# Seven products of sums of quarters in place of eight: the second matrix product of a gated feed-forward layer behind a packed attention

## The chip, the cores and the metric

The kernel runs on one core of one Trainium2 chip. The metric is the device time of one execution in microseconds, the median of three runs. Work is spread by hand over TensorE (PE, and PEld for its weight loads), VectorE (DVE), ScalarE (ACT) and the DMA queue that SyncE (SP) issues. GpSimd makes an identity matrix at the start and is idle after that.

## The reference, cut to what matters

```python
def sm_attn(qq, kk, vv):
    s = scale * np.matmul(qq, kk.transpose(0, 1, 3, 2))
    a = np.exp(s - np.max(s, axis=-1, keepdims=True))
    return np.matmul(a / (np.sum(a, axis=-1, keepdims=True) + 1e-09), vv)
# q, k, v: (8 batches, 8 heads, 576, 64); p: (8, 8, 32, 64)
p_packed = sm_attn(p, k, v)
x = sm_attn(q, p_packed, p_packed)      # as rows: (8 * 576, 512)
h = x @ w_in                            # w_in: (512, 2048)
g = h * np.tanh(np.log1p(np.exp(h)))    # mish
out = g @ w_out                         # w_out: (2048, 512)
```

All inputs come in 64 or 32 bits; the two weight matrices come as 64-bit floats and are turned into 32-bit ones in the kernel.

## The kernel before

A batch has 576 rows: four chunks of 128 and 64 left over. Since the attention has only 32 packed positions per head, w_in is first multiplied by the packed values (`pack`, L711), which gives 256 rows of weights for the batch, and the up product (`Group.up`, L800) multiplies these by the attention weights `aT`. Each of the 16 groups of a batch makes 128 of the 2048 hidden columns: two halves of 288 rows, six products each, since every operand stands as a high and a low part and three of the four cross products are kept. I call these products **ups**. ScalarE applies mish from PSUM to SBUF (`gate`, L810), VectorE makes the high part (`high`, L818) and the low part (`low`, L822).

The second product (`Group.down`, through `down_one`, L852 to L854) takes a 128x128 block of g as the stationary operand and 512 columns of w_out as the moving one. For each group and each of the four chunks it runs three products of 512 columns: high by high, high by low, low by high. I call these **downs**. Four PSUM banks hold the four chunks through the 16 groups of a batch; then `keep` (L841 to L845) copies each bank to SBUF and a DMA sends it. The 64 left rows of two batches are put side by side and multiplied by w_out once per four groups (`Left`, `ps_rest`, 48 products of 512 columns for a pair of batches).

w_out stays in SBUF all along as 16 tiles `wo` of high and low parts. w_in in 32 bits lies in DRAM (`w_in_f32`) and is fetched again for each batch.

Batches 0 and 1 run as three turns (half of batch 0, batch 1, the other half of batch 0), since the weights arrive and are converted during them; batches 2 to 7 run one after the other. The attention of the next batch (`later`) is interleaved with the groups of this one.

The order of instructions on every engine is fixed. The class `Lineup` is given each operation with an engine, an assumed cost, what it reads and which slots of which buffers it holds, and puts the operations in order; the kernel is written out in this order. Each engine runs its own list strictly in turn and waits where an operand or a buffer is late. The slots are named pools: `acc` (four PSUM banks for the second product), `ps_h`, `ps_x` and `ps_a` (PSUM for ups, scores and packs), `g` (mish output), `gs` (split g), `T`, `late`, `wstage`, `w32`.

## Time and profile before

| | |
|---|---|
| median of three runs | 721.99 us (721.77 to 722.18) |
| the profiled execution's own time | 722.63 us |
| its span, first to last instruction | 720.9 us |
| TensorE busy | 698.6 us, 97% of the span |
| VectorE busy | 394.4 us, 55% |
| ScalarE busy | 301.8 us, 42% |
| moved by DMA | 85.75 MB, mean 119 GB/s |

Busy time of TensorE is modelled: matmuls are pipelined and their recorded durations overlap, so the distance between two starts says what a product costs, and the chain of waits (what released what, followed back from the end) says how much of a stretch each line accounts for. An engine that is idle off that chain costs nothing.

### The profile page before, as it was taken

What the parts mean: (1) busy time and instruction counts of PE and PEld (TensorE: products, weight loads), DVE (VectorE), ACT (ScalarE), POOL (GpSimd) and SP (SyncE); (2) the same over time, 40 slices, a digit from 0 to 9 for tenths busy, and PEclk for the clock granted to TensorE, in tenths of its full rate; (3) what the DMA queues carried; (4) which work ended last, traced back from release to release, by engine and by line L of the source; (5) the groups of instructions that cost most, each with busy time, mean ns of one, the idle gap of its engine ahead of it and who ended that gap; (6) DMA issues with size and microseconds to landing.
All of it is one profiled execution on the core that took longest, in us unless ns stands there. A gap on an engine that the chain in (4) does not pass through costs nothing.

```text
span 720.9 us, 12533 instructions
## 1 busy us (share of the span) xinstructions
PE 698.6 (97%) x5050; PEld 571.4 (79%) x5050; DVE 394.4 (55%) x711; ACT 301.8 (42%) x718; POOL 0.7 (0%) x6
## 2 busy tenths in 40 slices
PE   5599999999999999999999999999999999999997
PEld 4278888777788788878888788887878878787885
DVE  5899878957544473355632555453643438332332
ACT  5598766565222443233422443334423344223211
POOL 0000000000000000000000000000000000000000
PEclk8879999999999999999999999999999999999999
DMA  9990255813047301641017310373016430130002
GB/s 316 363 371 3 88 150 203 292 60 117 5 135 256 118 1 59 207 159 75 1 59 282 129 43 1 108 273 117 1 26 220 150 117 1 59 117 1 1 1 73
DMA packets 29754, 85.75 MB, mean 119 GB/s; under 512 B 3584, under 2 KB 7680, under 8 KB 29696
## 3 DMA queue, kind: packets, MB, share of 16 engines
q1 hardware_dynamic: 29696, 84.95, 34.0%
q8 instruction: 40, 0.66, 0.4%
q14 instruction: 18, 0.15, 0.1%
HBM read 71.30 MB, written 13.63 MB: 118 GB/s over the span
## 4 chain that ended last, share of the span: by engine, by line
PE 93%; DMA 4%; ACT 1%; DVE 0%; issue 0%; SPq 0%
PE ps_h L800 28%; PE acc L852 17%; PE acc L853 16%; PE acc L854 16%; PE ps_w L711 4%; DMA xT<-in_k_main_dram 2%; PE ps_rest L852 2%; PE ps_rest L853 2%; PE ps_rest L854 2%; PE ps_m L302 1%; DMA w_st<-in_w_in_dram 1%; PE ps_pp L430 1%; PE ps_s L302 1%; DMA v_rest<-in_v_rest_dram 1%; PE ps_a L395 1%; PE ps_pp L445 0%
## 5 line engine op out<-in xcount | busy, mean ns | idle before, releaser
L810 ACT ACTIVATE g<-ps_h 128x288 f32<-128x288 f32 (+1 forms) x256 | 97.5, 386 | 310.6 <-PE ps_h L800 158.5
L852 PE MATMUL acc<-wo,g_hi 128*128 128x512 f32 x512 | 206.6, 404 | 0.0
L853 PE MATMUL acc<-wo,g_hi 128*128 128x512 f32 x512 | 202.2, 395 | 0.0
L854 PE MATMUL acc<-wo,g_lo 128*128 128x512 f32 x512 | 201.3, 393 | 0.0
L818 DVE CAST g_hi<-g 128x512 fp32r<-128x512 f32 x112 | 47.6, 425 | 212.5 <-PE acc L853 159.7
L800 PE MATMUL ps_h<-aT_hi,wp_hi 128*128 128x288 f32 x512 | 152.0, 297 | 0.3 <-ACT g L810 0.3
L800 PE MATMUL ps_h<-aT_hi,wp_lo 128*128 128x288 f32 x512 | 151.5, 296 | 0.0
L800 PE MATMUL ps_h<-aT_lo,wp_hi 128*128 128x288 f32 x512 | 151.4, 296 | 0.0
L852 PEld LDWEIGHTS acc<-wo,g_hi 128*128 128x128 f32 x512 | 96.2, 188 | 31.9 <-issue 20.1
L854 PEld LDWEIGHTS acc<-wo,g_lo 128*128 128x128 f32 x512 | 96.2, 188 | 22.5
L800 PEld LDWEIGHTS ps_h<-aT_hi,wp_hi 128*128 128x128 f32 x512 | 96.6, 189 | 13.4 <-issue 1.0
L853 PEld LDWEIGHTS acc<-wo,g_hi 128*128 128x128 f32 x512 | 96.3, 188 | 10.8
L800 PEld LDWEIGHTS ps_h<-aT_lo,wp_hi 128*128 128x128 f32 x512 | 96.7, 189 | 9.7
L800 PEld LDWEIGHTS ps_h<-aT_hi,wp_lo 128*128 128x128 f32 x512 | 96.6, 189 | 0.0
L822 DVE TENSOR_TENSOR g_lo<-g,g_hi 128x512 fp32r<-128x512 f32 x128 | 88.0, 688 | 9.0 <-DVE g_hi L818 0.5
L737 DVE TENSOR_TENSOR wp_lo<-ps_w,wp_hi 128x512 fp32r<-128x512 f32 x64 | 42.4, 686 | 14.7 <-ACT wp_hi L732 12.5
L732 ACT CAST wp_hi<-ps_w 128x512 fp32r<-128x512 f32 x64 | 35.3, 595 | 25.8 <-PE ps_w L711 24.9
L711 PE MATMUL ps_w<-wi,ppT 64*32 64x512 f32 x512 | 33.1, 597 | 0.0
L812 ACT ACTIVATE g_rest<-ps_h 128x64 f32<-128x64 f32 x128 | 28.5, 222 | 0.0
L852 PE MATMUL ps_rest<-wo,r_hi 128*128 128x512 f32 x64 | 25.1, 393 | 0.0
L853 PE MATMUL ps_rest<-wo,r_hi 128*128 128x512 f32 x64 | 25.1, 393 | 0.0
L854 PE MATMUL ps_rest<-wo,r_lo 128*128 128x512 f32 x64 | 25.1, 392 | 0.0
(96 smaller groups left out, 553.5 us busy)
## 6 DMA issues: line engine op xcount, KB each, us to landing
wi<-w_in_f SPq DMA_DIRECT2D x48, 512.0 KB, 5.1
w_st<-in_w_in_dram SPq DMA_DIRECT2D x16, 512.0 KB, 7.2
xT<-in_k_main_dram SPq DMA_DIRECT2D x16, 512.0 KB, 6.2
v<-in_v_main_dram SPq DMA_DIRECT2D x16, 512.0 KB, 6.6
xT<-in_q_main_dram SPq DMA_DIRECT2D x16, 512.0 KB, 7.5
w_st<-in_w_out_dram SPq DMA_DIRECT2D x16, 512.0 KB, 7.8
out_dram<-o SPq DMA_DIRECT2D x32, 256.0 KB, 2.2
w_in_f<-wi SPq DMA_DIRECT2D x8, 512.0 KB, 6.5
```

The costliest lines, as they stand in the source:

```text
L302: nc.tensor.matmul(out=out[u][h * NP:(h + 1) * NP], lhsT=packT[u * D:(u + 1) * D, h * NP:(h + 1) * NP], rhs=xT[u * D:(u + 1) * D, h * (e - ...
L711: nc.tensor.matmul(out=ps[g][h * NP:(h + 1) * NP], lhsT=ppTb[row:row + D, g, h * NP:(h + 1) * NP], rhs=wis[c, g][row:row + D, h // 2, :], ...
L732: nc.scalar.copy(out=hi, in_=fresh[b, c][g])
L737: nc.vector.tensor_tensor(out=lo, in0=fresh[b, c][g], in1=hi.bitcast(F32), op=ALU.subtract)
L800: nc.tensor.matmul(out=ps, lhsT=w[:, fs], rhs=a[:, g, cs], start=(n == 0), stop=(n == 5))
L810: nc.scalar.activation(out=self.act[:, hf * HALF:hf * HALF + m], in_=ps[:, :m], func=AF.Mish)
L812: nc.scalar.activation(out=self.g_rest[self.b % 2, self.f // 4][:, self.f % 4, :], in_=ps[:, m:], func=AF.Mish)
L818: cast(out=self.g[0], in_=self.act)
L822: nc.vector.tensor_tensor(out=lo, in0=self.act, in1=hi.bitcast(F32), op=ALU.subtract)
L852: nc.tensor.matmul(out=acc, lhsT=hi[:, cs], rhs=wh, start=start, stop=False)
L853: nc.tensor.matmul(out=acc, lhsT=hi[:, cs], rhs=wl, start=False, stop=False)
L854: nc.tensor.matmul(out=acc, lhsT=lo[:, cs], rhs=wh, start=False, stop=stop)
```

## The change

From batch 2 on (`PLAIN = 2`) the second product is made in steps. A step takes 256 rows (half of the four chunks of a batch) and 256 hidden columns, and sees g as 2x2 blocks of 128x128 and w_out as 2x2 blocks of 128x256. In place of eight block products it makes seven, of sums and differences of the blocks (the scheme of Strassen and Winograd), each as three products of 256 columns. The seven sums accumulate over the eight steps of a half batch in three and a half PSUM banks (`BANKS`), and at the end of the half batch eight operations (`ending`: one copy on ScalarE, seven additions on VectorE) combine them into two output chunks. I call the seven times three products of 256 columns of a step its downs as well.

For each step the ups of both hidden blocks run over 256 rows in the first half of a batch and over 320 in the second (256 and the left 64). VectorE then makes four sums of blocks in three operations (`sums`), ScalarE the high parts of seven blocks at once (`high`, 896 columns), VectorE their low parts (`low`, 896 columns).

The blocks of w_out and their differences are made once: the conversion also stores w_out in 32 bits and its quarters to DRAM, `Mix` reads it back, makes the differences, splits and stores them, and `fetch_mix` brings 512 KB tiles into 18 slots (`u`). A half batch uses 28 of them. Steps go through w_out forwards in one half and backwards in the next, so that 18 of the 28 stay across the turn and ten are fetched per half batch. The left rows use the same tiles (`LeftMixed`, 24 products of 256 columns each, for two row blocks at once).

Besides: the pools get other sizes (two slots `T` for k and q in place of four; v shares five slots with w_in; GB 4), the sign of a converted weight is taken by an operation with one tensor in place of one with two, and the exponentials of batches 2 to 7 are taken from PSUM with their sums on ScalarE, as batches 0 and 1 have it, in place of a subtraction, an exponential and a sum over SBUF.

```diff
-GB = 3
-PAIRS = 8
-STAGED = 100
-AHEAD = 0
-XB = 4
-VB = 2
+LATER = 3
+GB = 4
+PLAIN = 2
+XB = 2
+WV = 5
+UB = 18
+WB = 4
+SB = 4
...
-    wo = {i: const.tile([P, 2, DO], F32R, name=f"wo{i}") for i in range(NF // 2)}
+    wo = {}
...
+    mixed = [[dram.tile([P, 2, 2, DO // 2], F32, name=f"mixed{p}_{k}") for k in range(3)] for p in range(NF // 2)]
+    shared = [dram.tile([P, 2, 2, DO // 2], F32, name=f"shared{j}") for j in range(NF // 4)]
...
+        def sign(self):
+            self.r = wts.tile([P, FC], I32, name="wround", tag="w2k", bufs=W2K)
+            nc.vector.tensor_scalar(out=self.r, in0=self.high, scalar1=-0x80000000, scalar2=None, op0=ALU.bitwise_and)
...
+            low = self.r.bitcast(U16).rearrange("p (n t) -> p n t", t=2)[:, :, 0]
+            nc.scalar.activation(out=low, in_=self.lower.bitcast(U32), func=AF.Copy, scale=2.0 ** -29)
...
+        def keep_f32(self):
+            nc.sync.dma_start(out=w_out_f32[self.i // 2][:, self.i % 2], in_=self.dst)
...
+        def keep_quarters(self):
+
+            p, w, half = self.i // 2, wo[self.i], DO // 2
+            nc.sync.dma_start(out=mixed[p][2][:, self.i % 2], in_=w[:, :, :half].bitcast(F32))
+            if self.i % 2:
+                nc.sync.dma_start(out=shared[p // 2][:, p % 2], in_=w[:, :, half:].bitcast(F32))
...
+        def differences(self):
+            half = DO // 2
+            self.t = wts.tile([P, 4, half], F32, name="mix_t", tag="st", bufs=SB)
+            w, t = self.w.rearrange("p i (u m) -> p (i u) m", u=2), self.t
+            nc.vector.tensor_tensor(
+                out=t[:, 0:2], in0=w[:, 1:2].to_broadcast([P, 2, half]), in1=w[:, 0:4:3], op=ALU.subtract
+            )
+            nc.vector.tensor_tensor(out=t[:, 2], in0=w[:, 3], in1=t[:, 0], op=ALU.subtract)
+            nc.vector.tensor_tensor(out=t[:, 3], in0=w[:, 2], in1=t[:, 2], op=ALU.subtract)
...
+    def fetch_mix(p, k):
+        x = wts.tile([P, 2, 2, DO // 2], F32R, name="mix", tag="u", bufs=UB)
+        if k < 3:
+            mixes[p, k] = x
+            nc.sync.dma_start(out=x.bitcast(F32), in_=mixed[p][k])
+        else:
+            others[p // 2] = x
+            nc.sync.dma_start(out=x.bitcast(F32), in_=shared[p // 2])
...
+            for q in range(2):
+                for half, terms in enumerate((((0, "w11"), (1, "w21")), ((2, "w22"), (0, "t3")))):
+                    for m, (x, name) in enumerate(terms):
+                        three(
+                            self.ps[:, half * DO // 2:(half + 1) * DO // 2], self.hi[:, q, x], self.lo[:, q, x],
+                            quarter(2 * self.i + q, name), q == 0 and m == 0 and half == 0, q == 1 and m == 1 and half == 1,
+                        )
...
+    def three(acc, hi, lo, w, start, stop):
+
+        nc.tensor.matmul(out=acc, lhsT=hi, rhs=w[:, 0], start=start, stop=False)
+        nc.tensor.matmul(out=acc, lhsT=hi, rhs=w[:, 1], start=False, stop=False)
+        nc.tensor.matmul(out=acc, lhsT=lo, rhs=w[:, 0], start=False, stop=stop)
...
+        X = {"s4": 0, "s2": 1, "s3": 2, "s1": 3, "x12": 4, "x22": 5, "x11": 6, "x21": 7}
+        BANKS = (
+            (("x11", "w11"), ("x12", "w21")),
+            (("s2", "t2"), ("s3", "t3")),
+            (("s1", "t1"), ("s4", "w22")),
+            (("x22", "t4"),),
+        )
...
+            a, e = ((0, MAIN // 2), (MAIN // 2, S))[self.hf]
...
+        def sums(self):
+            x = self.x
+            nc.vector.tensor_tensor(out=x[:, 3], in0=x[:, 7], in1=x[:, 5], op=ALU.add)
+            nc.vector.tensor_tensor(
+                out=x[:, 1:3], in0=x[:, 3:8:4], in1=x[:, 6:7].to_broadcast([P, 2, P]), op=ALU.subtract
+            )
+            nc.vector.tensor_tensor(out=x[:, 0], in0=x[:, 4], in1=x[:, 1], op=ALU.subtract)
...
+            nc.scalar.copy(out=self.split[:, 0], in_=self.x[:, :7])
...
+            nc.vector.tensor_tensor(out=x[:, 1], in0=self.x[:, :7], in1=x[:, 0].bitcast(F32), op=ALU.subtract)
...
+            for n, (x, w) in enumerate(self.BANKS[k]):
+                at = self.X[x]
+                three(
+                    sums[k][:, n * DO // 2:(n + 1) * DO // 2], self.split[:, 0, at], self.split[:, 1, at],
+                    quarter(self.p, w), self.first and n == 0, self.last and n == len(self.BANKS[k]) - 1,
+                )
...
+            if n == 0:
+                nc.scalar.copy(out=k1, in_=m1)
+                return
+            out_, a, c = (
+                (o[0][:, 0], m2, k1), (u2, m6, k1), (u3, m7, u2), (u4, m5, u2), (o[1][:, 1], m5, u3),
+                (o[0][:, 1], m3, u4), (o[1][:, 0], m4, u3),
+            )[n - 1]
+            nc.vector.tensor_tensor(out=out_, in0=a, in1=c, op=ALU.add)
...
-    turns = TURNS + [(b, 0, NF) for b in range(2, B)]
+    turns = TURNS
...
+    steps = [
+        Step(b, hf, p if hf == 0 else NF // 2 - 1 - p, p == 0, p == NF // 2 - 1)
+        for b in range(PLAIN, B) for hf in range(2) for p in range(NF // 2)
+    ]
...
-                later(b, b < 2)
+                later(b, True)
...
+                elif at == 0:
+                    for p in range(5, 8):
+                        mixed_in(p, p == 6)
+                elif x.first:
+                    for p in (2, 1, 0):
+                        mixed_in(p, p == 1)
```

Three places in the order of instructions. TensorE near the start, between the second scores (`ps_s`) and the first ups (`ps_h`); `ps_t` are the transposes that turn the attention weights of batch 0, `ps_a` and `ps_pp` belong to the attention of batch 1. Before:

```order
L302 MATMUL ps_s_371<-xT,pT 32x320 x4
L545 MATMUL ps_t<-ident,a_310 128x128 x8
L395 MATMUL ps_a_454<-ident,a_366 128x128 x4
L395 MATMUL ps_a_455<-ident,a_366 128x128 x4
L399 MATMUL ps_a_454<-ident,a_366 128x128
L545 MATMUL ps_t<-ident,a_310 128x128
L430 MATMUL ps_pp<-v,a1T 32x64 x32
L445 MATMUL ps_pp<-v_rest,a1T_rest 32x64 x8
L800 MATMUL ps_h<-aT_hi,wp_hi 128x288
```

and now:

```order
L310 MATMUL ps_s_452<-xT,pT 32x256 x4
L310 MATMUL ps_s_453<-xT,pT 32x320 x4
L310 MATMUL ps_s_452<-xT,pT 32x256 x4
L310 MATMUL ps_s_453<-xT,pT 32x320 x4
L912 MATMUL ps_h<-aT_hi,wp 128x288
```

The first ups now stand right behind the scores of batch 1; the transposes and the values of batch 1 come after three halves of ups.

VectorE at the end of a batch before (the banks `acc_2499` and `acc_2501` are the two that VectorE copies):

```order
L818 CAST g_hi<-g 128x512
L822 TENSOR_TENSOR g_lo<-g,g_hi 128x512
L818 CAST g_hi<-g 128x512
L822 TENSOR_TENSOR g_lo<-g,g_hi 128x512
L845 COPY o<-acc_2499 128x512
L845 COPY o<-acc_2501 128x512
L818 CAST g_hi<-g 128x512
L822 TENSOR_TENSOR g_lo<-g,g_hi 128x512
```

and now at the end of the first half of batch 2 (`acc_2725`, `acc_2772`, `acc_2779` and `acc_2813` are its banks 0 to 3; `at` and `aT_lo` belong to the attention of batch 3):

```order
L1063 TENSOR_TENSOR o<-acc_2725,o 128x256
L622 STREAM_TRANSPOSE at<-a_3089 128x576
L1025 TENSOR_TENSOR x<-x 128x128
L1026 TENSOR_TENSOR x<-x 128x256
L1029 TENSOR_TENSOR x<-x 128x128
L1063 TENSOR_TENSOR o<-acc_2772,o 128x256
L631 TENSOR_TENSOR aT_lo<-at,aT_hi 128x576
L1063 TENSOR_TENSOR o<-acc_2772,o 128x256
L622 STREAM_TRANSPOSE at<-a_3089 128x576
L1063 TENSOR_TENSOR o<-acc_2779,o 128x256 x3
L631 TENSOR_TENSOR aT_lo<-at,aT_hi 128x576
L1063 TENSOR_TENSOR o<-acc_2813,o 128x256
```

In place of two copies stand seven additions, some of which read what an earlier one wrote, with parts of the attention and of the next step between them.

TensorE at the same turn, where `acc_3259` is bank 0 of the next half batch:

```order
L972 MATMUL acc_2772<-mix,mixed_split 128x256
L973 MATMUL acc_2772<-mix,mixed_split 128x256
L974 MATMUL acc_2772<-mix,mixed_split 128x256
L972 MATMUL acc_2779<-mix,mixed_split 128x256
L973 MATMUL acc_2779<-mix,mixed_split 128x256
L974 MATMUL acc_2779<-mix,mixed_split 128x256
L972 MATMUL acc_2779<-mix,mixed_split 128x256
L973 MATMUL acc_2779<-mix,mixed_split 128x256
L974 MATMUL acc_2779<-mix,mixed_split 128x256
L972 MATMUL acc_3259<-mix,mixed_split 128x256
L973 MATMUL acc_3259<-mix,mixed_split 128x256
L974 MATMUL acc_3259<-mix,mixed_split 128x256
```

The next half's first downs follow at once; bank 1 of the next half (`acc_3274`) comes 15 products behind the last one into `acc_2772`, bank 2 comes 27 behind the last one into `acc_2779`.

## Rows read from the trace of the kernel before

**Rows 1.** Windows by stage: per engine busy us (instructions), clock, DMA share, GB/s.
```profile
core 0: us, PE busy (x) PEld busy (x) DVE busy (x) ACT busy (x) POOL busy (x), PEclk, DMA share, GB/s
0.00:41.50 41.50, 24.66 (x326) 15.51 (x327) 29.39 (x68) 23.40 (x55) 0.70 (x6) 0.78 0.98 346
41.50:226.80 185.30, 184.75 (x1252) 151.20 (x1252) 136.13 (x247) 107.07 (x242) 0.00 (x0) 1.00 0.43 146
226.80:397.20 170.40, 170.40 (x1262) 140.53 (x1268) 83.70 (x146) 62.76 (x151) 0.00 (x0) 1.00 0.31 109
```

**Rows 2.** Chain that ended last, 226.8 to 397.2 us, by line.
```profile
by line: PE ps_h L800 29.8%; PE acc L852 18.6%; PE acc L853 17.5%; PE acc L854 17.4%; PE ps_w L711 4.4%; PE ps_rest L852 2.2%; PE ps_rest L853 2.2%; PE ps_rest L854 2.2%; PE ps_s L302 1.6%; PE ps_m L302 1.5%; PE ps_pp L430 1.2%; PE ps_a L39
```

**Rows 3.** Groups by form: times run, busy us, mean ns, idle before.
```profile
L852 PE MATMUL acc<-wo,g_hi 128*128 128x512 f32 x512 | 206.6, 404 | 0.0
L800 PE MATMUL ps_h<-aT_hi,wp_hi 128*128 128x288 f32 x512 | 152.0, 297 | 0.3 <-ACT g L810 0.3
L800 PEld LDWEIGHTS ps_h<-aT_lo,wp_hi 128*128 128x128 f32 x512 | 96.7, 189 | 9.7
```

**Rows 4.** Timeline at 247.63 us: start us, us, what.
```profile
247.63 1.03 PE L395 MATMUL ps_a<-ident,a 128*128 128x128 f32 x8
248.51 0.27 PE L399 MATMUL ps_a<-ident,a 128*128 128x128 f32 x1
```

**Rows 5.** Groups by form: the work behind an up and at batch's ends.
```profile
L818 DVE CAST g_hi<-g 128x512 fp32r<-128x512 f32 x112 | 47.6, 425 | 212.5 <-PE acc L853 159.7 <-ACT g_rest L812 37.4 <-ACT g L810 11.2
L822 DVE TENSOR_TENSOR g_lo<-g,g_hi 128x512 fp32r<-128x512 f32 x128 | 88.0, 688 | 9.0 <-DVE g_hi L818 0.5
L605 DVE TENSOR_TENSOR aT_lo<-ps_t,aT_hi 128x128 fp32r<-128x128 f32 x1 | 0.3, 283 | 0.0
L760 DVE TENSOR_TENSOR r_lo<-g_rest,r_hi 128x256 fp32r<-128x256 f32 x32 | 12.1, 419 | 7.0 <-ACT r_hi L756 7.0
L508 DVE TENSOR_TENSOR a<-a,small 128x1152 f32<-128x1152 f32 x7 | 9.5, 1357 | 0.2
L810 ACT ACTIVATE g<-ps_h 128x288 f32<-128x288 f32 x128 | 53.0, 414 | 217.7 <-issue 147.2 <-PE ps_h L800 65.7 <-ACT wp_hi L732 2.9
L818 ACT CAST g_hi<-g 128x512 fp32r<-128x512 f32 x16 | 10.2, 637 | 1.5 <-PE acc L853 1.4
L618 ACT CAST aT_hi<-at 128x576 fp32r<-128x576 f32 x14 | 9.4, 675 | 6.8 <-DVE at L612 6.8
```

**Rows 6.** Timeline before the first up, 31.16 to 41.50 us.
```profile
31.16 1.42 DVE L588 TENSOR_TENSOR a<-a,small 128x512 f32<-128x512 f32 x2
32.95 0.67 ACT L645 ACTIVATE wi<-w_st 128x512 f32<-128x512 f32 x1 [3.35 <-DMA w_st<-in_w_in_dram]
...
35.60 1.97 PE L395 MATMUL ps_a<-ident,a 128*128 128x128 f32 x8 [1.68 <-ACT a L364]
37.73 0.42 DVE L652 TENSOR_SCALAR wi<-wi 128x512 f32<-128x512 f32 x1
40.48 0.28 DVE L605 TENSOR_TENSOR aT_lo<-ps_t,aT_hi 128x128 fp32r<-128x128 f32 x1
41.50 0.61 PE L800 MATMUL ps_h<-aT_hi,wp_hi 128*128 128x288 f32 x1
```

**Rows 7.** The page's DMA: rate by slice of 18 us, queue, landing.
```profile
GB/s 316 363 371 3 88 150 203 292 60 117 5 135 256 118 1 59 207 159 75 1 59 282 129 43 1 108 273 117 1 26 220 150 117 1 59 117 1 1 1 73
q1 hardware_dynamic: 29696, 84.95, 34.0%
wi<-w_in_f SPq DMA_DIRECT2D x48, 512.0 KB, 5.1
```

**Rows 8.** Timeline of the end.
```profile
715.66 0.39 PE L854 MATMUL acc<-wo,g_lo 128*128 128x512 f32 x1
716.08 0.69 DVE L845 COPY o<-acc 128x512 f32<-128x512 f32 x1 [0.67 <-PE acc L854]
716.20 1.52 SPq L848 DMA_DIRECT2D out_dram<-o  x3
```

More of the change, by code (lines that the diff above doesn't have):

```diff
@@ L836, in keep @@
             elif before is None:
-                o = parts[b, c] = wts.tile([P, DO], F32, name=f"part{b}{c}", bufs=1)
+                if c % 2 == 0:
+                    halves[b, c // 2] = wts.tile([P, 2, DO], F32, name="part", tag="u", bufs=UB)
+                o = parts[b, c] = halves[b, c // 2][:, c % 2]
             else:
@@ L1114, in packed, with again @@
                     add("ACT", 480, lambda g=g, m=m: pack_high(m, g), reads=[("pw", m)], writes=[("wph", m, g)],
-                        takes=[(pack_place(m), ("wp", m, g))], uses=[banks[m][g][0][1]])
+                        takes=[(pack_place(m), ("wp", m, g))], uses=[banks[m][g][0][1]],
+                        behind=mixing[0] if two else None)
                     add("DVE", 605, lambda g=g, m=m: pack_low(b, chunks[m][1], g), reads=[("wph", m, g)], writes=[("wp", m)],
                         uses=[banks[m][g][0][1], ("wp", m, g)])
+            if two and last_up[0] is not None:
+                line.follow(last_pack[0], last_up[0])
             return last_pack[0]
-        def again(n):
-            add("SP", 900, lambda: fetch_wi(chunks[n][1]), never_before=due(4 * n - 8), reads=[("stored", chunks[n][1])],
-                writes=[("again", n)], takes=[("w32", ("wi", n, g)) for g in range(2)], lag=wire(P * 8192))
+        def again(n, when):
+            held[0] = add("SP", 900, lambda: fetch_wi(chunks[n][1]), never_before=when, reads=[("stored", chunks[n][1])],
+                writes=[("again", n)], takes=[("wv", ("wr", n, g)) for g in range(2)], lag=wire(P * 8192), behind=held[0])
         def block(t):
@@ L1188, in converted @@
+        refetched = [any(c == x[1] for x in chunks[:n]) for n, (b, c) in enumerate(chunks)]
+        made, pair, versions, fetched = [0], [None], {}, [None]
         def converted(n):
@@ L1200, in program, with pack_pair @@
         loads(1)
-        for t in range(len(order) + LAG):
-            for b in range(1, B):
-                if t == max(first_of[b] - 16, 0):
-                    if b > 1:
-                        loads(b, due(first_of[b] - LOAD))
-                    attention(b)
+        def pack_pair(b, c, when):
+            n = simple + 4 * (b - PLAIN) + c
+            for m in (n, n + 1):
+                if c == 0:
+                    again(m, when)
+            pair[0] = packed(n)
+            if c == 0:
+                for m in (n + 2, n + 3):
+                    again(m, when)
+        for t in range(len(order) + LAG):
+            if t == 0:
+                attention(1)
             n = t // 4
-            if t % 4 == 0 and n < min(PAIRS, len(chunks)):
+            if t % 4 == 0 and n < simple:
                 if refetched[n]:
-                    again(n)
+                    again(n, due(4 * n - 8))
                 else:
@@ L1213, in program @@
                 packed(n)
-            n = (t + AHEAD) // 4
-            if (t + AHEAD) % 8 == 0 and PAIRS <= n < len(chunks):
-                for m in (n, n + 1):
-                    if refetched[m]:
-                        again(m)
-                    else:
-                        converted(last_wi[chunks[m][1]])
-                pair[0] = packed(n)
+            if t == len(order) - 12:
+                loads(PLAIN, due(t - 3))
+                attention(PLAIN)
+            if t == len(order) - 4:
+                for p in range(NF // 2):
+                    mix(p)
+            if t == len(order) - 3:
+                pack_pair(PLAIN, 0, due(t - 3))
             if t < len(order):
```

310 lines of the change are left out of this document (252 added, 58 removed).

## The prediction

> **What bounds the kernel now.** I read the windows by stage first [rows 1]. Up to 41.5 us TensorE is busy for 24.66 us only, and the DMA engines for 98% of the time: this is loading. From then on TensorE fills every window (170.40 of 170.40 us in a pair of batches at a granted clock of 1.00, which is 2.4 GHz), while VectorE has 83.70 us of work, ScalarE 62.76, and the DMA engines are 31% busy. Then the chain of waits of the same pair of batches [rows 2]: 29.8% of it are ups, 18.6 + 17.5 + 17.4% downs, and what is left are other TensorE products; no wait for another engine has a noticeable share. So a product removed is time removed, as long as the engines behind it keep up. The groups by form [rows 3] say nothing of a product's price: 404 ns for 512 columns overlaps its neighbours. The chain's shares do.
>
> **What a product costs.** A pair of batches has 32 groups: times 12 that makes 384 ups of 288 columns, and times 4 chunks 128 downs of each of the three kinds. L853 and L854 hold 34.9% of 170.4 us, which over 256 products gives 0.2323 us for 512 columns; 29.8% over 384 gives 0.1322 us for 288 columns [rows 2]. A straight line through both has 0.447 ns a column and 3.5 ns besides: 0.1179 us for 256 columns, 0.1465 us for 320. No product of 256 columns with a new stationary operand each time stands in this trace, so this is the unknown cost. Its lower bound: eight transposes of 128 columns, each with its own load, start 0.88 us before the next row [rows 4], 0.110 us each. Its upper bound: the 288-column product, 0.1322 us. I take the line, since both its ends are long streams of loads and products of the same kind and 256 lies next to 288.
>
> **The change, part by part.** Batches 2 to 7 alone change in their downs: 6 x 16 groups x 4 chunks x 3 = 1152 products of 512 columns go, 267.6 us. Six batches x 2 halves x 8 steps = 96 steps of 21 products = 2016 products of 256 columns come, 2016 x 0.1179 = 237.7 us. That is **-29.9 us**. The left rows: 3 x 48 = 144 products of 512 columns (33.5 us) become 12 x 24 = 288 of 256 (34.0), **+0.5 us**. The ups: 1152 of 288 columns (152.3 us) become 576 of 256 and 576 of 320 (152.3 by the same line), **0**.
>
> The start, **-2.5 us**, between 0 and -4.5. Before, the transposes of batch 0 and the attention of batch 1 run on TensorE from 35.60 us and the first up starts at 41.50, right behind the last aT_lo at 40.48 [rows 6]. The order of now puts the first ups right behind the scores of batch 1, and aT_lo needs only VectorE's transposes. VectorE's last softmax operations of batch 0 end at 32.6 us; in its order of now five operations of 0.42 us and one of 0.28 [rows 6] and three of 0.69 [rows 5] lead from there through aT_lo, 4.4 us, so the first up could start near 37 us. Against that, w_in arrives late already (ScalarE waits 3.35 us for it at 32.95 us [rows 6]), and the ups only go on if weights are converted, in a stretch (41.5 to 226.8 us) where VectorE has 136 of 185 us of work [rows 1]. I take somewhat more than half of the 4.5 us.
>
> The turns of half batches, **+4 us**, between 0 and 20. Before, banks are emptied by copies of 512 columns. Now there are 12 half batches, each with eight operations at its end that read banks, and the next half takes bank 1 again 15 products after its last one, 15 x 0.118 = 1.77 us. In VectorE's order two additions that read bank 1 have an aT_lo of 576 columns between them: additions of 256 columns take 0.419 us [rows 5], the aT_lo by the line through 128 and 512 columns (283 and 688 ns) 0.755 us, together 1.59 us; VectorE's start after the last product took 0.42 us at the end of the kernel (715.66 to 716.08 [rows 8], with the product itself). So bank 1 comes free between 1.6 and 2.0 us, and bank 2 has 27 products (3.2 us) for a transpose of 576 columns and three more additions (some 2 us on top). This is a wait of 0 to 0.8 us per turn; 12 x 0.35 is my 4 us, and 12 x 1.7 us, if VectorE comes late from a step before, the 20. Behind a down that waits for a bank stands all of TensorE's order, the next ups too.
>
> The chain inside a step costs nothing, since it is covered: up, gate (0.414 us for 288 columns), three sums (0.283 + 0.419 + 0.283), high part of 896 columns on ScalarE (0.675 for 576, so 0.86 to 1.05), low part (688 ns at 512 columns, 1357 at 1152, so 1.09) [rows 5], some 3.6 us and about 4.1 with the passes between engines. In TensorE's order mostly 75 to 150 products, 9 to 18 us by the prices above (a product takes 0.118 to 0.132), stand between a step's last up and its first down. If that cover were gone, each of the 96 steps would pay up to 4.1 us.
>
> The engines' load per pair of batches: VectorE 83.7, less 32 x (0.425 + 0.688) = 35.6 for the present high and low parts, plus 32 x 2.08 = 66.5, plus 28 endings of 0.419 = 11.7, less the two subtractions of 1.357 us, makes 124 us of the 156 that TensorE will need, 79%. ScalarE gets 32 x 0.96 = 31 us more, 94 us, 60%. Making the differences is extra: for each of eight pairs about 2.9 us of VectorE and 1.3 of ScalarE by the same rows, 23 and 10 us, inside 41.5 to 226.8 us where VectorE has 49 us idle [rows 1].
>
> DMA: the moved bytes go from 85 MB [rows 7] to about 185: 138 fetches of 512 KB are 72 MB, the stored and read forms of w_out some 27. A batch of the later ones needs about 19.4 MB; at 371 GB/s, the best slice [rows 7], 52 us of the 78 that the batch takes. A fetch of 512 KB lands 5.1 us after its issue [rows 7], and in the orders of SP and TensorE its slot mostly comes free some four steps, 4 x 4.9 us, before its tile is read. So it costs nothing while SP, which issues in order, is not held by a fetch whose slot is late; then outputs and loads behind it are late too.
>
> The end stays as it is: the last product, one VectorE operation, one store [rows 8].
>
> **Sum.** The profiled execution took 722.6 us, span 720.9. 722.6 - 29.9 + 0.5 - 2.5 + 4 = 694.7 us; the median is 0.6 below the profiled execution, so **694 us**.
>
> **A page that speaks against it.** The eight transposes [rows 4] had 110 ns each for load and product together. The Trainium skill, "TensorE: Matmul & The Clock Gate", section "Back-to-back issue gap", says that in a stream of pairs of load and product both set the spacing: 81 ns at 128 columns where the product alone would take about 56. By it, 25 ns more on the 109 ns of a lone 256-column product are an estimate of 134 ns, and the change would lose. The same section gives 131 ns at 512 columns, where this trace has 232; there the measurement decides.
>
> **Rivals.**
> (a) The forecast, 686 to 702 us: 62%.
> (b) Cheaper products. If 256 columns cost exactly half of 512 (0.1162), 2880 products (2016 + 288 + 576 ups) save 4.9 us more, 689; at the transposes' 0.110 another 17.9 us, 671. For it speaks that the short transposes have 0.110 for half of the columns; against it that this figure is nowhere near proportional. 9%, between 676 and 686.
> (c) The vector engines hold the downs: at 79% VectorE needs only one delayed operation in front of an ending. 12 turns of 1.7 us, or 96 steps of 0.15 us, give 702 to 714. For it speaks that additions and parts of the attention share VectorE's order at the turn; against it that 9 to 18 us of products stand in front of nearly every other wait. 14%.
> (d) The fetches hold it: if SP stands behind a late slot once per half batch for 0.5 to 2 us, 12 x 2 = 24 us, and the left products early in batch 2 wait for the last differences: 700 to 720. Against it: 31% DMA share now [rows 1], about 67% then. 10%.
> (e) The other side: the stationary load sets a floor. Each product has a load of its own, recorded with 189 ns [rows 3], nearly two thirds of its 297 ns product at 288 columns. If a product can't be shorter than the 288-column one, 0.1322 us, then 2880 x 14.3 ns = 41 us come on top: 735 us, slower. It decides where the whole gain of 28 us is eaten, at 28 / 2880 = 9.7 ns more a product, 0.1276 us. Against it: load and product of 128 columns fit into 0.110 us [rows 4], so that no floor above that exists, and 288 and 512 columns lie on a line with almost no constant. 5%.
>
> **How the numbers follow.** The predicted time is case (a)'s. Case (b) below 684 and cases (c) to (e) above 710 hold some 2 in 10 together: the range is 684 to 710. About 0.2% (1.4 us) is what a measurement of this kernel can tell from no change. Slower is (e) with one part in a hundred of (c) and (d): 0.06; within 0.2% 0.04; faster 0.90.
>
> **What the profile of the changed kernel would show.** Products of 256 columns 0.118 us apart in a stretch of downs, ups of 320 0.146 us. A pair of batches some 156 us long, TensorE still full in it, the chain still over 90% TensorE. The first up near 39 us. Idle time of TensorE ahead of the downs into bank 1 and 2 at the turns, released by VectorE, 0.3 us each. VectorE near 80% and ScalarE near 60% in the later batches, DMA share about 0.6. Wrong would be: the spacing above 0.1276 us (case e); TensorE's wait before downs named as the low part of g (c), or as a DMA into the tiles of w_out (d).

## The result, and the profile after

The changed kernel takes 714.14 us (median of 4 runs, 711.99 to 715.96), the kernel before beside it 722.09: ratio 0.9898, interval 0.9885 to 0.9911. It is faster, by 8 us in place of 28, and lies above the range. Its profiled execution has a span of 712.8 us, 8.1 less than before.

The windows of the changed kernel, columns as in [rows 1]:

```profile
core 0: us, PE busy (x) PEld busy (x) DVE busy (x) ACT busy (x) POOL busy (x), PEclk, DMA share, GB/s
0.00:41.50 41.50, 23.46 (x249) 14.83 (x249) 28.19 (x68) 23.37 (x52) 0.70 (x6) 0.87 0.97 354
41.50:60.00 18.50, 17.71 (x198) 14.10 (x199) 13.03 (x27) 15.38 (x37) 0.00 (x0) 0.82 1.02 376
100.00:150.00 50.00, 48.60 (x299) 38.77 (x298) 40.81 (x84) 33.32 (x76) 0.00 (x0) 1.00 0.99 341
150.00:200.00 50.00, 47.97 (x385) 38.34 (x384) 36.60 (x66) 23.39 (x51) 0.00 (x0) 1.00 0.95 343
200.00:227.00 27.00, 25.61 (x167) 20.92 (x166) 17.74 (x33) 12.59 (x29) 0.00 (x0) 1.00 0.76 285
305.00:384.00 79.00, 78.90 (x776) 73.80 (x773) 58.03 (x124) 45.01 (x101) 0.00 (x0) 1.00 0.71 249
540.00:618.00 78.00, 77.46 (x763) 72.23 (x763) 53.51 (x106) 42.41 (x90) 0.00 (x0) 1.00 0.61 228
```

In the later batches TensorE is as full as before (78.90 of 79.00), with VectorE at 73% and ScalarE at 57%. What is new stands between 100 and 227 us: TensorE is idle for 1.40, 2.03 and 1.39 us in the three windows, and the DMA engines, 43% busy in that stage before [rows 1], are 99, 95 and 76% busy. In the chain of waits of 305 to 384 us, which answers to [rows 2], everything is still TensorE:

```profile
by line: PE ps_h L1008 29.0%; PE acc L972 17.7%; PE acc L973 16.7%; PE acc L974 16.7%; PE ps_w L780 4.8%; PE ps_rest L972 2.4%; PE ps_rest L973 2.4%; PE ps_rest L974 2.4%; PE ps_s L310 1.9%; PE ps_m L310 1.6%; PE ps_pp L438 1.3%; PE ps_a L4
```

The timeline near the end shows the price of a product of 256 columns (first column: start in us):

```profile
704.84 0.28 PE L972 MATMUL ps_rest<-mix,r 128*128 128x256 f32 x1
704.96 0.28 PE L973 MATMUL ps_rest<-mix,r 128*128 128x256 f32 x1
705.08 0.28 PE L974 MATMUL ps_rest<-mix,r 128*128 128x256 f32 x1
...
705.92 0.28 PE L972 MATMUL acc<-mix,mixed_split 128*128 128x256 f32 x1
```

Starts are 0.120 us apart; 0.1179 was forecast. Ups of 320 columns measure 0.1467 in the same way, of 288 0.132 to 0.133 (0.1322 on average in the kernel before).

To say where time went I add up, over a stretch, the distances between neighbouring starts on TensorE less the price of each product in an undisturbed stretch (0.1200, 0.1333, 0.1467 and 0.2323 us for 256, 288, 320 and 512 columns, the small products by their own rows), and call it **lost time**. Up to 60 us it is 28.1 us before and 31.1 after; from there to the first step's downs (231.4 us; before, to 227 us) 1.9 and 8.8; from there to the end about 0 and 6.7. The first of these numbers is the least sure: kernels whose TensorE starts with the same products as the changed one's differ by 1.5 us in it.

Three places in the changed kernel show what is in it. First the start, timeline, TensorE and ScalarE (in brackets the idle time before the row, and what ended it):

```profile
34.62 0.40 PE L912 MATMUL ps_h<-aT_hi,wp 128*128 128x288 f32 x1
37.71 0.47 ACT L372 ACTIVATE a<-ps_s,top 128x256 f32<-128x256 f32 x1 [4.50 <-DVE top L360]
38.78 0.61 PE L912 MATMUL ps_h<-aT_hi,wp 128*128 128x288 f32 x1 [3.11 <-ACT a L372]
40.32 1.28 ACT L922 ACT_TABLE_LOAD   x1
42.08 0.61 PE L912 MATMUL ps_h<-aT_hi,wp 128*128 128x288 f32 x1 [1.49 <-ACT g L922]
```

The first up starts 6.9 us earlier than before. But the second half of ups wants a PSUM bank that the scores of batch 1 hold until the exponentials (L372) have read it, and these wait 4.50 us for VectorE's row maxima (L360). The third half waits for the gate, behind a table load. Between 38 and 42 us TensorE is busy for 1.8 of 4 us, and the granted clock stays at 0.50, the 1.2 GHz level, until 48 us; before, it was back at 1.00 from 44 us. The windows, the changed kernel first, then the kernel before:

```profile
40.00:48.00 8.00, 6.30 (x24) 5.12 (x24) 5.26 (x14) 6.68 (x13) 0.00 (x0) 0.50 1.03 364
48.00:60.00 12.00, 12.00 (x179) 9.22 (x179) 9.16 (x19) 10.19 (x25) 0.00 (x0) 1.00 1.02 381
```

```profile
40.00:44.00 4.00, 4.00 (x73) 3.66 (x65) 4.00 (x9) 2.31 (x4) 0.00 (x0) 0.58 1.02 409
44.00:60.00 16.00, 15.74 (x127) 12.47 (x126) 15.47 (x28) 13.85 (x35) 0.00 (x0) 1.00 0.56 222
```

Second, the differences, at 151 us, VectorE, ScalarE and TensorE:

```profile
151.43 0.69 DVE L726 TENSOR_TENSOR mix_t<-mix_w 128x512 f32<-128x512 f32 x1 [1.78 <-DMA mix_w<-w_out_f]
...
153.08 0.62 ACT L734 CAST mix_o<-mix_t 128x512 fp32r<-128x512 f32 x1 [3.35 <-DVE mix_t L730]
...
153.71 1.28 ACT L922 ACT_TABLE_LOAD   x1
...
155.01 0.66 ACT L922 ACTIVATE g<-ps_h 128x288 f32<-128x288 f32 x2
...
155.47 0.40 PE L912 MATMUL ps_h<-aT_hi,wp 128*128 128x288 f32 x1 [1.66 <-ACT g L922]
```

VectorE stands 1.78 us in front of w_out read back; ScalarE stands behind VectorE for 3.35 us; the gate of an up whose last product started at 150.3 us stands behind both, and TensorE waits for its bank. At 202 us the same happens once more (1.31 us lost), with packed weights (w_in times the packed values, L799 and L804) in place of the gate:

```profile
199.28 0.69 DVE L726 TENSOR_TENSOR mix_t<-mix_w 128x512 f32<-128x512 f32 x1 [3.07 <-DMA mix_w<-w_out_f]
...
203.66 0.37 PE L912 MATMUL ps_h<-aT_hi,wp 128*128 128x288 f32 x1 [1.16 <-DVE wp L804]
```

SyncE is held as well. From 140 to 203 us it waits 20.9 us in front of stores of differences (L743) whose low part is not ready, and the reads of the next pairs are issued from the same queue, in turn (us in all, times, longest):

```profile
SPq L743 <- DVE mix_o L738: 20.9, 7, 5.9
```

Third, the one long wait at a turn, at 472 us:

```profile
472.30 0.16 DVE L377 TENSOR_TENSOR rs<-sums 128x2 f32<-128x2 f32 x1 [3.47 <-ACT a L372]
...
472.78 1.41 DVE L1063 TENSOR_TENSOR o<-acc,o 128x256 f32<-128x256 f32 x4
473.68 0.36 PE L972 MATMUL acc<-mix,mixed_split 128*128 128x256 f32 x1 [1.40 <-DVE o L1063]
```

The additions did not take too long: they stood for 3.47 us behind a row of 0.16 us of the next batch's softmax that waited for ScalarE's exponentials. Of twelve turns this is the only one with such a wait in this execution.

### The profile page after: what moved, and what is told of

Its sections match the earlier page's. It is cut to its first block, busy times and chain, and to the rows that moved or that the text cites. A ratio compares the mean times of both kernels' runs of the same rounds, so it can differ in the third digit from the quotient of the medians.

```text
span 712.8 us, 15348 instructions
## 1 busy us (share of the span) xinstructions
PE 680.6 (95%) x6058; PEld 610.2 (86%) x6058; DVE 507.7 (71%) x1033; ACT 401.9 (56%) x884; POOL 0.7 (0%) x6
## 4 chain that ended last, share of the span: by engine, by line
PE 76%; DMA 10%; DVE 8%; ACT 4%; SPq 1%; issue 1%; DVEq 0%; ACTq 0%
PE ps_h L1008 21%; PE acc L972 12%; PE acc L973 11%; PE acc L974 11%; DMA mix_w<-w_out_f 5%; PE ps_w L780 3%; PE ps_h L912 3%; PE ps_rest L974 2%; PE ps_rest L973 2%; PE ps_rest L972 2%; DMA xT<-in_q_main_dram 1%; PE acc L966 1%; PE ps_m L310 1%; PE acc L967 1%; PE acc L968 1%
## 5 line engine op out<-in xcount | busy, mean ns | idle before, releaser
L972 PE MATMUL acc<-mix,mixed_split 128*128 128x256 f32 x672 | 192.8, 287 | 1.5 <-DVE o L1063 1.4
L973 PE MATMUL acc<-mix,mixed_split 128*128 128x256 f32 x672 | 190.1, 283 | 0.0
L974 PE MATMUL acc<-mix,mixed_split 128*128 128x256 f32 x672 | 190.0, 283 | 0.0
L1008 PE MATMUL ps_h<-aT_hi,wp 128*128 128x256 f32 (+1 forms) x768 | 174.9, 298 | 1.3 <-ACT a1T L429 1.0
L1037 DVE TENSOR_TENSOR mixed_split<-x,mixed_split 128x896 fp32r<-128x896 f32 x96 | 104.4, 1088 | 55.9 <-ACT mixed_split L1033 54.3
L972 PEld LDWEIGHTS acc<-mix,mixed_split 128*128 128x128 f32 x672 | 128.5, 191 | 14.8 <-issue 12.0
L1033 ACT CAST mixed_split<-x 128x896 fp32r<-128x896 f32 x96 | 90.4, 942 | 83.1 <-DVE x L1029 30.8
L1008 PEld LDWEIGHTS ps_h<-aT_hi,wp 128*128 128x128 f32 x768 | 131.1, 190 | 3.9 <-ACT a1T L429 1.7
L974 PEld LDWEIGHTS acc<-mix,mixed_split 128*128 128x128 f32 x672 | 128.9, 192 | 0.0
L973 PEld LDWEIGHTS acc<-mix,mixed_split 128*128 128x128 f32 x672 | 128.7, 191 | 0.0
L1014 ACT ACTIVATE x<-ps_h 128x256 f32<-128x256 f32 x192 | 73.4, 384 | 97.3 <-PE ps_h L1008 97.0
L1008 PE MATMUL ps_h<-aT_lo,wp 128*128 128x320 f32 (+1 forms) x384 | 113.6, 296 | 0.0
L1008 PEld LDWEIGHTS ps_h<-aT_lo,wp 128*128 128x128 f32 x384 | 73.0, 190 | 0.2
L912 PEld LDWEIGHTS ps_h<-aT_hi,wp 128*128 128x128 f32 x256 | 44.5, 193 | 16.3 <-issue 4.6
L804 DVE TENSOR_TENSOR wp<-ps_w,wp 128x512 fp32r<-128x512 f32 x64 | 41.5, 684 | 15.8 <-ACT wp L799 15.6
L966 PE MATMUL acc<-wo,split 128*128 128x512 f32 x128 | 51.6, 403 | 0.0
L967 PE MATMUL acc<-wo,split 128*128 128x512 f32 x128 | 50.5, 395 | 0.1
L968 PE MATMUL acc<-wo,split 128*128 128x512 f32 x128 | 50.4, 393 | 0.0
L799 ACT CAST wp<-ps_w 128x512 fp32r<-128x512 f32 x64 | 34.0, 596 | 16.5 <-PE ps_w L780 15.2
```

Of the source, the lines that this page charges most:

```text
L804: nc.vector.tensor_tensor(out=lo, in0=fresh[b, c][g], in1=hi.bitcast(F32), op=ALU.subtract)
L912: nc.tensor.matmul(out=ps, lhsT=w[:, fs], rhs=a[:, g, cs], start=(n == 0), stop=(n == 5))
L966: nc.tensor.matmul(out=acc, lhsT=hi[:, cs], rhs=wh, start=start, stop=False)
L967: nc.tensor.matmul(out=acc, lhsT=hi[:, cs], rhs=wl, start=False, stop=False)
L968: nc.tensor.matmul(out=acc, lhsT=lo[:, cs], rhs=wh, start=False, stop=stop)
L972: nc.tensor.matmul(out=acc, lhsT=hi, rhs=w[:, 0], start=start, stop=False)
```

## The experiments

All times stand against the changed kernel's 714.1 us, which was measured apart from them; the kernel before took 721.5 to 721.9 beside them, 722.1 beside the changed kernel. Where a wait or a stall is told, it is of one profiled execution.

**The price of a product.** Eight series behind the last product:

```diff
+        w = mixes[0, 0].rearrange("p n t m -> p (n t m)")
+        for n, cols in enumerate((512, 384, 320, 288, 256, 192, 128, 64)):
+            ps = single("ps_width", FC)
+            for i in range(21):
+                nc.tensor.matmul(out=ps[:, :cols], lhsT=steps[-1].split[:, 0, i % 7], rhs=w[:, :cols], start=True, stop=True)
```

> Adds, behind the last product, eight series of 21 products on TensorE, of 512, 384, 320, 288, 256, 192, 128 and 64 columns, each with a load of its own, into a bank that nothing reads. Theory: columns / 2.4 GHz plus 13.3 ns, so 0.2267, 0.1733, 0.1467, 0.1333, 0.1200, 0.0933 us and so on. Rival 1: the line of the prediction, 0.447 ns a column and 3.5 ns, 0.1179 at 256 and 0.0893 at 192. Rival 2: a floor of the load, so that 192 and 128 columns take no less than 0.100 us.

Measured, for three of the series: their first row and a later one, timeline in short windows.

```profile
720.39 0.50 PE L1594 MATMUL ps_width<-mix,mixed_split 128*128 128x256 f32 x2
...
722.52 0.64 PE L1594 MATMUL ps_width<-mix,mixed_split 128*128 128x256 f32 x4
723.22 0.47 PE L1594 MATMUL ps_width<-mix,mixed_split 128*128 128x192 f32 x2
...
725.20 0.61 PE L1594 MATMUL ps_width<-mix,mixed_split 128*128 128x192 f32 x4
...
728.49 0.41 PE L1594 MATMUL ps_width<-mix,mixed_split 128*128 128x64 f32 x2
...
730.41 0.61 PE L1594 MATMUL ps_width<-mix,mixed_split 128*128 128x64 f32 x4
```

17 products start between the two rows of 256 columns, 2.13 us; the first distance of a series is longer (0.22 us here), the other 16 are 0.119 us. In the same way: 512 columns 0.228, 384 0.174, 320 0.147, 288 0.132, 256 0.119, 192 0.112, 128 0.112, 64 0.112. From 256 to 384 columns it is columns / 2.4 GHz and 12 to 13 ns, at a granted clock of 1.00; from 192 columns down there is a floor of 0.112 us. Theory and rival 2 were both half right. The 0.110 us of the transposes [rows 4] lies next to this floor. The forecast's 0.1179 came out too low because neither end of its line fits columns / 2.4 GHz and 13 ns: 512 columns lie 1 to 6 ns above (0.228 here, 0.2323 in the kernel before), 288 columns about 1 ns below (0.132).

**An eighth product in each step**, into the half bank that nothing reads:

```diff
-            (("x22", "t4"),),
+            (("x22", "t4"), ("x11", "t1")),
```

> An eighth product of quarters (three products of 256 columns more in each of 96 steps, into the half bank that no ending reads). Theory: from batch 2 on TensorE is still what bounds the changed kernel, so 288 products at the spacing that its trace shows, 0.1200 us, come on top in full: 714.1 + 34.6 = 748.7 us, between 746 and 751. Rival: part of the lost gain went into waits on VectorE, ScalarE and DMA, which longer steps would cover: then well under 34.6 us more, 735 to 744.

744.53 us, +30.4. This lies between theory and rival: by price the products are 34.6 us, and lost time fell by 3.2 us up to the first downs (the order there came out differently) and by 2.7 after; 34.6 - 5.9 = 28.7 against 27.9 between the spans.

**No differences; and their transfers alone:**

```diff
 # no differences
-                for p in range(NF // 2):
-                    mix(p)
...
-            nc.sync.dma_start(out=x.bitcast(F32), in_=mixed[p][k])
+            nc.sync.dma_start(out=x.bitcast(F32), in_=mixed[p][2])
...
 # transfers alone: L726 to L738 go, and
-            nc.sync.dma_start(out=mixed[self.p][k], in_=self.o[k].bitcast(F32))
+            nc.sync.dma_start(out=mixed[self.p][k], in_=self.w.rearrange("p i (u m) -> p i u m", u=2))
```

> Leaves out the making of the differences: no read back, no subtraction, no split, no store of them, and no 32-bit copy of w_out; the tiles fetched in their place are w_out's first quarters, so the output is that of other weights. Theory: TensorE loses 6.6 us more than before between 60 and 230 us because ScalarE and VectorE stand in order behind a difference whose read has not landed; without it 714.1 - 6 = 708 us, between 706 and 710. Rival: these waits come from the conversion of the weights and from the attention, which stay: 713 to 715.

> Keeps every transfer of the differences (the 32-bit copy, the reading back, two stores for each pair), but VectorE and ScalarE do nothing for them: what is read is stored again as it is, so the output is that of other weights. Theory (the wait for a transfer inside the engines' order costs, and nothing queues behind the read any more): nearly the whole gain of the kernel without differences, 707 to 711 us. Rival: the DMA engines' load itself is what costs, since other reads land late: 712 to 715.

The first took 711.75 us, below the rival and above the theory: the stalls from 142 us on went (0.5 us left of 4.3 in single stalls), but some 3 us came up at 97 to 104 us, where the conversion of weights had come into another order. The total says little; the place of the gain is the theory's. The second took 707.29, as the theory had it. Two of its windows:

```profile
100.00:150.00 50.00, 48.19 (x301) 39.26 (x301) 34.59 (x73) 31.71 (x71) 0.00 (x0) 1.00 1.02 383
150.00:200.00 50.00, 50.00 (x409) 40.96 (x408) 27.10 (x46) 20.35 (x50) 0.00 (x0) 1.00 0.98 369
```

The DMA engines are as full as in the changed kernel, and TensorE has no idle time from 150 to 200 us. So full DMA engines are not the cause by themselves; the engines' part of the chain is. Which piece of it is not parted: this run takes away some 32 us of work on VectorE and ScalarE, the 6.9 us that VectorE waits in front of the reads and the 14.0 us that ScalarE waits behind VectorE, three of the four staging slots that a pair holds, and SyncE's waits in front of the stores, all at once. Nor do the whole 6.8 us belong to the differences: about 5 us of lost time go between 60 us and the first step, 1 us goes before that, which the spread of the start alone can make, and 1 us after.

**The start: old order, and ups ahead of the scores:**

```diff
 # old order: ups behind the values of batch 1
                 attention(1)
+                pair[0] = line.writers[("pv", 1)][0]
 # ups first
-            if t == 0:
+            if t == 1:
                 attention(1)
+                line.follow(line.writers[("s", 1)][0], last_up[0])
```

> TensorE's first ups are put behind the transposes and values of batch 1, as before the change; nothing else is asked for. Theory: the early ups gained nothing, since their second bank was held by the scores of batch 1 until the exponentials had read it, and the thin stretch kept the granted clock at 0.50 until 48 us; the old order gives a first up near 41 us, full clock from about 44 us, and 711 to 713 us. Rival: starting early is worth what the prediction had, 2 to 3 us, and this kernel takes 716 to 717.

> The scores of batch 1 are put behind the two halves of the first ups, so that these ups do not wait for a bank that the scores hold. Theory: the wait of 3.1 us at 38.8 us goes, and the clock has no second thin stretch: 710 to 713 us, unless the later attention of batch 1 holds the second turn. Rival: TensorE then waits elsewhere before 60 us (for converted weights), 713 to 715.

719.55 and 745.6 us: both theories fell. In the old order the first up starts at 44.96 us, lost time up to 60 us is 32.3, and 2.7 us more are lost after that. So the early ups were no loss, and the loss at the start is there without them. The 745.6 us hold one stall of 15.7 us at 211 us, behind packed weights (L804): the place of the differences again. The start did not gain either: the wait for the exponentials only moved, to 44.71 us (2.27 us).

**Two slots for k and q, in the kernel before, alone:**

```diff
-XB = 4
+XB = 2
```

> The kernel before, with two slots for k and q in place of four and nothing else. Theory: in the changed kernel the k of batch 1 waits for a slot until batch 0's scores are done (issued at 22 us in place of 15), so its scores stand at 32.5 in place of 24.7 us, the exponentials hold the second bank of the ups, and the clock stays at 0.50 until 48 us; two slots alone do the same to the kernel before, and put 3 to 6 us on it: 725 to 728 us. Rival: the late scores come from the loads' new order or from v's sharing of slots with w_in, and this kernel takes 721 to 723.

724.5 us, ratio 1.0037 (1.0024 to 1.0049): +2.7, a little under the theory. SyncE's rows for k of batch 1 (of the kernel before, of this one, of the changed one):

```profile
15.44 0.35 SPq L276 DMA_DIRECT2D xT<-in_k_main_dram  x1
```

```profile
21.41 0.33 SPq L276 DMA_DIRECT2D xT<-in_k_main_dram  x1
```

```profile
22.11 0.33 SPq L285 DMA_DIRECT2D xT<-in_k_main_dram  x1
```

With two slots, k of batch 1 waits for a slot; its scores stand at 30.67 us (32.47 in the changed kernel, 24.68 before), and lost time up to 60 us is 32.1, as bad as in the changed kernel (31.1), with the clock at 0.50 from 40 to 48 us as well. The order of instructions is made anew for two slots, and here too the first ups come early and thin:

```profile
33.45 0.38 PE L800 MATMUL ps_h<-aT_hi,wp_hi 128*128 128x288 f32 x1
```

So the smaller pool is shown as a cause of the loss at the start, together with the order that follows from it. The changed kernel with four slots was not tried.

**The differences later in the order, and in place:**

```diff
 # later
-                ends[n] = wire + self.LATE
+                ends[n] = wire + op.get("late", self.LATE)
...
+            line.ops[n]["late"] = 8000
 # in place: no mix_t, differences go to the low halves of the stored tiles
-            self.t = wts.tile([P, 4, half], F32, name="mix_t", tag="st", bufs=SB)
+            self.o = [wts.tile([P, 2, 2, half], F32R, name="mix_o", tag="st", bufs=SB) for _ in range(2)]
+            t, s = (o.bitcast(F32)[:, :, 1] for o in self.o)
```

> The operations that need a tile of w_out read back are put 6 us later in the engines' order (the order is made as if the read landed 8 us after its place in the queue, in place of 2). Nothing else changes. Theory: ScalarE and VectorE no longer stand in front of a read that has not landed; TensorE's stalls at 153 and 202 us (1.8 and 1.3 us) go, 709 to 712 us. Rival: the differences are then late for the first steps, or the stalls come from elsewhere: 714 or more.

> The differences of a pair are written straight into the tiles that are stored (into their low halves, split in place), so that a pair needs three staging slots in place of four; instructions, their sizes and the transfers stay. Theory: the eight pairs form a chain, one pair in flight since four slots are all there are, and each link waits for its read; with a slot left the next read is under way earlier and the two stalls at 153 and 202 us (1.8 and 1.3 us) go: 709 to 712 us. Rival: the read is late because the DMA engines are full (0.95 to 0.99 busy there), and a free slot changes nothing: 713 to 716.

> The same kernel again, one look, beside the next one on the same chip: 709 to 712 us by the theory of the free slot, 713 to 716 by its rival.

734.11, 725.49 and 724.75 us: the theory of these runs fell. The first removed the two stalls and made one of 18.9 us:

```profile
212.55 0.69 DVE L726 TENSOR_TENSOR mix_t<-mix_w 128x512 f32<-128x512 f32 x1 [5.47 <-DMA mix_w<-w_out_f]
...
214.24 1.14 ACT L734 CAST mix_o<-mix_t 128x512 fp32r<-128x512 f32 x2 [7.88 <-DVE mix_t L730]
...
215.28 0.58 ACT L799 CAST wp<-ps_w 128x512 fp32r<-128x512 f32 x1
...
216.93 0.58 PE L912 MATMUL ps_h<-aT_hi,wp 128*128 128x288 f32 x1 [18.87 <-DVE wp L804]
```

The last pair's read comes late, the differences behind it, then the packed weights of batch 2 (L799, L804), half of which have their place in SBUF among the four staging slots, so that they stand behind all differences. Until they are read, they hold both PSUM banks of the ups. With the differences in place the same stall is 10.0 us, at 199 us: SyncE issues the read of a pair behind other rows of its queue that wait, and a slot that is free sooner does not move it.

**The packs of batch 2 (the products that make its packed weights) behind the last plain ups (those of batches 0 and 1):**

```diff
-            if t == len(order) - 3:
+            if t == len(order):
                 pack_pair(PLAIN, 0, due(t - 3))
```

> The changed kernel with the first packs of batch 2 on TensorE behind the last ups of the plain batches, in place of ahead of the last ups. Theory: the stall of 1.3 us at 202 us goes, and little else changes: 711 to 714 us. Rival: TensorE then waits for these packs ahead of the first step, 714 to 718.

> The kernel whose differences come 6 us later in the engines' order (734.1 us, 18.9 us of it in one stall at 198 us), now with the packs of batch 2 behind the last plain ups. Theory: the packs held both banks of the ups until the chain of differences ended; the ups of the plain batches can now go on, and most of the stall is gone: 714 to 722 us. Rival: the chain itself is late, and the same wait stands in front of the first step: 728 to 735.

> The kernel with the differences in place (725.5 us, 10.0 us of it in one stall at 199 us), now with the packs of batch 2 behind the last plain ups. Theory: most of the stall goes, 714 to 718 us. Rival: it moves, 723 to 726.

713.41, 735.95 and 731.16 us. The first can't be told from the changed kernel (its runs, 712.26 to 714.74, lie among the others): the stall at 202 us went, and stalls of 2.30 us at 152 us and 1.07 us at 184 us stand in its profile. In the second and third the stall only moved, as the rivals had it, though both times lie above the rivals' ranges. In the second it stands in front of the first step:

```profile
231.24 0.55 PE L1008 MATMUL ps_h<-aT_hi,wp 128*128 128x256 f32 x1 [17.23 <-DVE wp L804]
```

In the third it stands behind the first step's downs, at 225 us, and shows what the packed weights wait for, a staging slot that the store of a difference still holds:

```profile
228.96 0.59 ACT L799 CAST wp<-ps_w 128x512 fp32r<-128x512 f32 x1 [9.82 <-DMA mixed<-mix_o]
...
234.19 1.96 PE L780 MATMUL ps_w<-wi,ppT 64*32 64x512 f32 x16 [8.77 <-issue]
```

So the banks are where TensorE feels it, and the chain of eight pairs (read, differences, high part, low part, store) is what is late. The landing of the last pair's read goes with the stall behind the packed weights: 183.1 us with transfers alone (no stall), 199.3 in the changed kernel (1.2 us), 204.4 with the differences in place (10.0), 212.5 with them later in the order (18.9). In the changed kernel the last low part ends at 203 us, 1.3 us after TensorE needs what stands behind it. Whether packed weights with slots of their own would free TensorE from the chain was not tried.

**The exponentials as before:**

```diff
-                later(b, True)
+                later(b, b < 2)
```

> For batches 2 to 7 the exponentials are made as before the change (subtraction on VectorE, exponential on ScalarE, sums on VectorE). Theory: the one long wait at a turn (1.4 us at 473.7 us) goes, since the additions at the turn no longer stand behind VectorE's wait for the exponentials; some 2 us at most, 712 to 714. Rival: VectorE, 71% busy, gets 4.1 us more in each batch, and the turns wait longer: 716 to 720.

> Differences in place as in the run before, the read of a pair placed right behind the differences of the pair before it, and the exponentials of batches 2 to 7 as before the change. Theory: two separate gains add up, since with the old exponentials TensorE lost 2.9 us from batch 2 on in place of 6.7, and lost its time before that (3.6 us in one stall at 202 us) to the chain of the differences, which the free slot shortens: 705 to 710 us. Rival: VectorE's extra work in the stretch of the differences takes it back: 712 to 716.

> The changed kernel with the exponentials of batches 2 to 7 as before the change (715.1 us, 3.6 us of it in one stall at 202 us) and the packs of batch 2 behind the last plain ups. Theory: the stall goes and the 3.8 us that the old exponentials bring from batch 2 on are left: 709 to 712 us. Rival: 714 to 716.

715.08, 717.48 and 710.9 us. In the first, lost time from the first downs on falls from 6.7 to 2.9 us, and no wait at a turn is left; one stall of 3.6 us at 202 us takes it back. The second, with the differences in place and the reads asked for earlier, has 7.3 us there, and its theory fell with that of the in-place runs. The third has the packs behind the ups as well. Three of its windows:

```profile
200.00:227.00 27.00, 27.00 (x189) 20.78 (x188) 18.21 (x34) 10.73 (x23) 0.00 (x0) 1.00 0.90 331
227.00:540.00 313.00, 312.50 (x3061) 292.08 (x3060) 232.45 (x472) 174.55 (x363) 0.00 (x0) 1.00 0.72 257
540.00:618.00 78.00, 78.00 (x754) 74.65 (x753) 58.39 (x113) 43.74 (x89) 0.00 (x0) 1.00 0.61 230
```

TensorE is idle for 0.50 of the 418 us from 200 to 618 us. The ratio is 0.9851 (0.9836 to 0.9865); this is the shortest of all runs that leave no work out, and clear of the changed kernel's interval (0.9885 to 0.9911). Neither of its two edits alone was clear of it.

## Why the prediction was wrong

What was right: TensorE bounds the kernel before and after, a product's price is paid nearly in full (30.4 of 34.6 us for the eighth), the chain inside a step and the fetches of tiles are hidden in the changed kernel (from 231 us on no row of TensorE waits for a high or low part or a tile), and the end did not change. The direction followed from that. The size failed at four terms of the sum.

**The price of a product of 256 columns** was mis-sized. 0.1200 in place of 0.1179 us on 2016 + 288 + 576 products is 6 us; with 0.1467 for 320 columns, downs, left rows and ups change by -25.7 + 1.1 + 1.3 = -23.3 us, where -29.4 was forecast. The line's two ends lie on either side of what the other widths follow. Rival (e) named a floor, and one exists, with another height: 0.112 us, 8 ns under this product. That the load sets it is not shown, since no series ran without loads. The Trainium skill, "TensorE: Matmul & The Clock Gate", section "LDWEIGHTS (loading the stationary operand)", has columns / 1.2 GHz for a load; 107 ns for 128 columns is an estimate by it, 5 ns under the measured floor. The 81 and 131 ns that the Trainium skill gives for 128 and 512 columns in the same page's section "Back-to-back issue gap" are not what was measured here (112 and 228).

**The start** has the wrong sign: +3.0 us of lost time in place of -2.5. I followed aT_lo alone, and it came even earlier than I said. I did not follow the bank that the second half of ups needs, nor what the smaller pool of k and q does to the scores of batch 1. That pool, with the order made for it, puts 2.7 us on the kernel before.

**"Making the differences is extra [...] inside 41.5 to 226.8 us where VectorE has 49 us idle"** is the step that failed worst: 6.9 us more were lost in this stretch, against nothing. I compared amounts of work, but it is a chain of eight reads, each with several steps on engines that keep their order, while the DMA engines are 95 to 99% busy; 49 us of idle time did not shorten it. With the engines' part left out and the transfers kept, about 5 of these 6.9 us go; what the other 2 are stays open.

**The turns** were forecast at 4 us for the wrong reason. I priced the additions; the rows show one wait of 1.4 us, behind a softmax row that waits for ScalarE. From the first downs on 6.7 us are lost, 3.8 of them with the exponentials on ScalarE. Single waits of TensorE explain 2.6 us (1.5 for the additions, 1.1 for a1T, the turned attention weights that ScalarE copies); the rest are small pieces that I can't name.

Sum: -23.3 + 3.0 + 6.9 + 6.7 = -6.7 us against -8.1 between the spans. Of the gap of 1.4 us, 1.3 come from two prices for one product: the -23.3 takes an up of 288 columns at 0.1322 us, the lost times take it at 0.1333, over 1152 ups. With 0.1333 in both, the products change by -24.6 us and the sum is -8.0. Of the rivals, (c) and (d) came nearest in time (702 to 714, 700 to 721). Of what (c) describes, a delayed operation in front of an ending, one case is there, the 1.4 us; of (d) none in the changed kernel, where no row of TensorE waits for a fetched tile.

What stays open: whether a shorter chain of differences (computed from the converted weights, without reading them back) would bring the 5 us; it wasn't tried.

## What to carry to other kernels

Price a product of a new width by a neighbour in width, and ask for the floor of a product: half of 512 columns cost 0.120 in place of 0.116 us here, and half of 256 would still cost 0.112. Work that is "extra on an idle engine" is to be priced as a chain, from its first read to what waits for its last result, with every queue that it passes and every buffer that it shares. When buffers are made smaller to make room, follow each load that used them to its new issue time, to the bank or operand that it fills, and to what TensorE does in the meantime.

## What was not expected of the hardware

A TensorE product with a new stationary operand of 128 columns takes 0.112 us at 64, 128 and 192 columns alike. Between 256 and 384 columns it takes columns / 2.4 GHz and 12 to 13 ns, at a granted clock of 1.00.

With TensorE busy for 1.8 of the 4 us from 38 to 42 us, the granted clock stayed at 0.50 until 48 us in the changed kernel; in the kernel before, with TensorE busy all through from 40 to 44 us, it was at 1.00 from 44 us on. An early first up is not needed for this: in the run with the old order the first up starts at 44.96 us, and the clock is at 0.50 until 46 us all the same. In the kernel with a stall of 18.9 us the first ups behind it start 0.24 us apart at a granted clock of 0.50, against 0.133 at 1.00.
